# Second layer by Strassen's scheme, exp in eight pieces, and a written-out order, in a fused attention and two-layer kernel

## The chip, the cores and the metric

The kernel runs on one core of one Trainium2 chip. The metric is the device time in microseconds (us) of a launch; each kernel is run several times and the median is given.

## The reference

Attention in chunks of 64 tokens, then two dense layers with a leaky ReLU between them. 8 sequences of 576 tokens, 8 heads of 64; the layers take 4608 tokens of 512 features to 2048 and back to 512.

```python
def _attn_ref(q, k, v):                      # (8, 8, 576, 64)
    scores = scale * np.matmul(q_c, k_c.transpose(0, 1, 2, 4, 3))    # per chunk of 64 tokens
    scores = scores - np.max(scores, axis=-1, keepdims=True)
    attn = np.exp(scores)
    attn = attn / (np.sum(attn, axis=-1, keepdims=True) + 1e-09)
    out = np.matmul(attn, v_c)
...
def _moe_ref(x, w_in, w_out):                # (4608, 512), (512, 2048), (2048, 512)
    h = x @ w_in
    g = np.maximum(0.01 * h, h)
    return (g @ w_out).astype(np.float32)
```

Inputs and output are float32 in memory; on the chip everything that TensorE reads behind the first unit is 16-bit float (f16), and sums are float32.

## The kernel before, in words

The attention runs over 36 units of 128 tokens (two chunks, eight heads). A unit u passes through these stages, each a small function: queries and keys in transposed form (`stage_dq`, `stage_dk`: VectorE transposes 32x32 blocks of a tile loaded by POOL's queue, for units from 9 on; `stage_tq`, `stage_tk`, `stage_q`, `stage_k` before that), scores (`stage_s`: eight TensorE matmuls of 64 columns into the PSUM tile `Sp`, L342), row maximum (`stage_m`, VectorE, L351), subtraction of it (`stage_b`, VectorE, L355), one exp over all 512 elements (`stage_x`, ScalarE, L361), row sums, plus 1e-9 and reciprocal (`stage_z`, VectorE, L367 to L371), normalisation (`stage_n`, VectorE, L376), transposition (`stage_d`, a transposing DMA on SP's queue, L398, for units from 5 on), value matmuls (`stage_v`, eight of 64 columns, L409) and copy to `xT` (`stage_a`, ScalarE, L422).

The layers run over 17 blocks of tokens: eight of 128, four of 256, five of 512. The first layer (`mm1`) fills one PSUM bank of 512 columns for each chunk; `act1` takes it out through the leaky ReLU on ScalarE into `gT` (L181). The second layer (`mm2`) goes over tiles of 128 tokens, with 16 matmuls of 512 columns for each, in four chunks; `store` copies the tile out on ScalarE (L202) and sends it off on SP's queue. The last tile is split in three (`last`).

Every engine works through its instructions in the order in which the program issues them. That order is written out by hand: `FRONT` for the beginning (to unit 5), and then a loop in which each iteration issues the stages of several units, with chunks of the layers between them (`fill`; `QUARTERS` says how many). PSUM has eight banks: one for `Sp`, one each for `qp` and `kp` (the early transposes), one (`ox`) for the transposed weights and the values, and four (`mm`) that the layers rotate through.

Of the kernel before, what the change touches and what calls it, by code (L numbers as in the profile page):

```python
# [16 lines left out]
def kernel(  # L17
# [15 lines left out]
    CH = 64  # L33
# [8 lines left out]
    UD = 9  # L42
    UE = 5
    G = 2 * CH
# [13 lines left out]
    xT = sbp.tile([128, NT, n_tok], FP16, name="xT")  # L58
    qk: dict[int, tuple[bass.AP, bass.AP]] = {}

# [21 lines left out]

    qkd: dict[int, tuple[bass.AP, bass.AP]] = {}
# [67 lines left out]

    gT: dict[int, bass.AP] = {}
# [6 lines left out]
    def mm1(j, a):  # L159
# [3 lines left out]
        for i in range(nf):  # L163
            fc = nf * a + i
            for t in range(NT):
                nc.tensor.matmul(  # L166
                    out=hT[:, i, :],
                    lhsT=w_inT[:, t, fc * 128:(fc + 1) * 128],
                    rhs=xT[:, t, r0:r0 + tb],
                    start=(t == 0),  # L170
                    stop=(t == NT - 1),
                )
        HT[j, a] = hT

    def act1(j, a):
        tb = BLOCKS[j]
        nf = 512 // tb
        if j not in gT:
            tag, bufs, pad = ("gS", 4, 128) if tb == 128 else ("gT", 2, 512)
# [20 lines left out]
    def store(j, ti):  # L200
        osb = sbp.tile([128, d_model], FP32, name="osb", tag="osb", bufs=3)
# [4 lines left out]
    def last(j, ti):  # L206
        r0 = START[j] + ti * 128
        osb = sbp.tile([128, d_model], FP32, name="osb", tag="osb", bufs=3)
# [26 lines left out]

    chunks = []
    for j in range(len(BLOCKS)):
        chunks += c1(j) + c2(j)
    state = {"tokens": 0}

    def fill(n):
        for _ in range(n):
            if not chunks:
                return
            kind, j, a, p = chunks[0]
            if START[j] + BLOCKS[j] > state["tokens"]:
                return
            chunks.pop(0)
            if kind == "mm1":
                mm1(j, a)  # L250
                act1(j, a)
            elif j == len(BLOCKS) - 1 and a == BLOCKS[j] // 128 - 1:
                if p == 0:
                    last(j, a)
            else:
                mm2(j, a, p)
                if parts[j, a] == NFC // 4:
                    store(j, a)


# [97 lines left out]

    def stage_x(u):
# [5 lines left out]
    def stage_z(u):  # L365
        z = sbp.tile([128, 8], FP32, name="z", tag="z", bufs=2)
        nc.vector.tensor_reduce(out=z, in_=E[u], axis=AXL.X, op=ALU.add)  # L367
# [52 lines left out]
    def stage_a(u):  # L420
        xp = XP.pop(u)
        nc.scalar.activation(out=xT[:, :, u * G:(u + 1) * G], in_=xp, func=AFT.Copy, bias=0.0, scale=1.0)  # L422
# [17 lines left out]
    def finish(j):  # L440
        store(j, 0)
# [11 lines left out]
    def zero_act(i):  # L453
# [22 lines left out]
        "I": identity,  # L476
# [24 lines left out]
    def values(u):  # L501
        if 0 <= u < NU:
            do("v", u)
            do("a", u)

    QUARTERS = [5, 5, 5, 5, 5, 5, 6, 5, 6, 7, 6, 5, 9, 6, 7, 6, 6, 4, 6, 7, 5, 8, 7, 7, 9, 7, 4, 9, 4, 7, 7, 7, 7, 7, 7, 7, 7, 7, 7, 7, 7, 7, 7, 7, 7, 7, 7, 7, 7]
    for it in range(6, NU + 3):
        dve = UD <= it < NU
        if it <= NU:
            do("s", it - 1)  # L510
            do("m", it - 1)
            do("b", it - 1)
        if dve:
            stage_dq(it, 0)
        fill(2)
        if it - 3 >= UE:
            values(it - 3)
        if it <= NU:
            do("x", it - 1)
        if it - 2 < UE:  # L520
            do("e", it - 2)
            do("c", it - 2)
        if dve:
            stage_dq(it, 1)
            stage_dk(it)
        elif it < UD:
            do("tq", it)
            do("tk", it)
            both(it)
            do("k", it)  # L530
        if it <= NU:
            do("z", it - 1)
            do("n", it - 1)
            if it - 1 >= UE:
# [39 lines left out]
```

## Time and profile before

| | |
|---|---|
| median of 3 runs | 292.17 us (292.0 to 292.24) |
| span of the profiled execution | 290.8 us |
| time beyond the span (median less span) | 1.37 us |
| TensorE busy | 283.5 us, 97% of the span |
| VectorE busy | 178.4 us, 61% |
| ScalarE busy | 154.4 us, 53% |
| POOL busy | 118.5 us, 41% |
| mean granted TensorE clock | 0.994 |

The profile follows one execution; its own total time is not listed apart from the three runs, so the span stands beside their median. PE is TensorE's matmuls and PEld its weight loads, DVE is VectorE, ACT is ScalarE, SP and POOL are the engines whose queues issue most DMAs. A row of grouped instructions gives line, engine, operation, output and input tiles, shapes, count, busy time, the mean length of one in ns, and the idle time in front of them with what ended it. L166 is line 166 of the kernel before.

### The profile page before, as it was taken

How to read it: one execution, taken by the hardware profiler on the slowest of the kernel's cores; microseconds unless marked ns; L12 is line 12 of the kernel's file. 1: busy time of each engine (PE TensorE's matmuls, PEld its weight loads, DVE VectorE, ACT ScalarE, POOL GpSimd, SP SyncE). 2: the span in 40 equal slices, each digit the busy share in tenths (PEclk: the TensorE clock that was granted, in tenths of full speed). 3: DMA queues.
4: the chain of work that ended last, by engine and by line, in shares of the span. 5: the costliest groups of instructions: out<-in, count | busy, mean ns of one | idle time of the engine just before them, and what ended most of it. 6: DMA issues, size and time to landing. Idle time of an engine off the chain costs nothing.

```text
span 290.8 us, 6052 instructions
## 1 busy us (share of the span) xinstructions
PE 283.5 (97%) x2468; PEld 170.4 (59%) x2468; DVE 178.4 (61%) x333; ACT 154.4 (53%) x273; POOL 118.5 (41%) x148
## 2 busy tenths in 40 slices
PE   8789999999999999999999999999999999999995
PEld 4579945877776767667454444445454444444444
DVE  5866245778968899989776797987777520000000
ACT  6756524575564564555575347733773377126511
POOL 8748545697735944961393359500000000000000
PEclk9979999999999999999999999999999999999999
DMA  9999999999999999999599799993201210010012
GB/s 149 158 195 155 177 177 190 159 119 166 161 132 116 148 115 175 110 125 155 68 143 99 78 158 149 92 126 95 70 18 54 92 54 2 36 75 34 2 72 72
DMA packets 191580, 32.51 MB, mean 112 GB/s; under 512 B 182593, under 2 KB 187073, under 8 KB 191553
## 3 DMA queue, kind: packets, MB, share of 16 engines
q0 software_dynamic: 167136, 18.10, 119.3%
q1 hardware_dynamic: 23232, 13.70, 20.4%
q10 hardware_dynamic: 1184, 0.33, 0.5%
q8 instruction: 19, 0.31, 0.4%
q14 instruction: 9, 0.07, 0.1%
HBM read 36.70 MB, written 9.44 MB: 159 GB/s over the span
## 4 chain that ended last, share of the span: by engine, by line
PE 92%; DMA 3%; POOL 2%; issue 0%; DVE 0%; DVEq 0%; POOLq 0%
PE hT L166 43%; PE oP L191 42%; DMA w_inT<-in_moe_w_in_dram 3%; PE xp L409 3%; PE Sp L342 3%; PE oP L217 1%; POOL VB L103 1%; POOL k_in L79 1%; POOL q_in L79 1%; PE kp L276 0%; PE qp L276 0%; PE tpe L384 0%; POOL w_inT L110 0%; DVE osb L225 0%; POOL ident masks.py:199 0%
## 5 line engine op out<-in xcount | busy, mean ns | idle before, releaser
L166 PE MATMUL hT<-xT,w_inT 128*128 128x128 f16 (+2 forms) x1088 | 133.6, 279 | 0.4 <-DMA w_inT<-in_moe_w_in_dram 0.3
L191 PE MATMUL oP<-w_outT,gT 128*128 128x512 f16 x560 | 128.4, 379 | 0.0
L166 PEld LDWEIGHTS <-w_inT 128*128 128x128 f16 x1088 | 83.6, 98 | 38.4 <-issue 0.6
L181 ACT ACTIVATE gT<-hT 128x512 f16<-128x512 f32 x144 | 84.0, 598 | 35.6 <-PE hT L166 35.0
L191 PEld LDWEIGHTS <-gT 128*128 128x128 f16 x560 | 52.4, 98 | 56.5
L202 ACT ACTIVATE osb<-oP 128x512 f32<-128x512 f32 x35 | 20.9, 596 | 67.4 <-PE oP L191 62.5
L94 POOL DMA_DIRECT2D q_d<-in_q_dram x48 | 38.8, 822 | 33.3 <-DVE QZ L324 27.5
L351 DVE TENSOR_REDUCE mx<-Sp 128x8 f32<-128x512 f32 x36 | 24.8, 688 | 31.6 <-PE Sp L342 31.3
L94 POOL DMA_DIRECT2D k_d<-in_k_dram x48 | 38.9, 842 | 3.5 <-DMA q_d<-in_q_dram 3.0
L324 DVE STREAM_TRANSPOSE QZ<-q_d 64x512 f16<-64x512 f16 (+1 forms) x60 | 38.2, 644 | 0.4
L422 ACT ACTIVATE xT<-xp 128x512 f16<-128x512 f32 x36 | 21.4, 594 | 23.0 <-PE xp L409 23.0
L225 DVE COPY osb<-oP 128x128 f32<-128x128 f32 x1 | 0.3, 291 | 53.7 <-PE oP L217 53.7
L367 DVE TENSOR_REDUCE z<-ex 128x8 f32<-128x512 f16 x36 | 23.6, 656 | 5.4 <-ACT ex L361 5.1
L103 POOL DMA_DIRECT2D VB<-in_v_dram x16 | 18.5, 1172 | 18.1 <-PE xp L409 17.1
L376 DVE TENSOR_TENSOR en<-ex,zi 128x512 f16<-128x512 f16 x36 | 24.9, 691 | 1.2
L355 DVE TENSOR_TENSOR sh<-Sp,mx 128x512 f32<-128x512 f32 x36 | 24.8, 690 | 1.1
L361 ACT ACTIVATE ex<-sh 128x512 f16<-128x512 f32 x36 | 22.5, 626 | 1.1 <-DVE sh L355 1.1
L332 DVE STREAM_TRANSPOSE KT<-k_d 128x512 f16<-128x512 f16 (+1 forms) x30 | 19.4, 654 | 2.2 <-DMA k_d<-in_k_dram 1.4
L409 PEld LDWEIGHTS <-VB 128*128 128x128 f16 x288 | 13.2, 99 | 6.7 <-issue 0.9
L342 PEld LDWEIGHTS <-QZ 128*128 128x128 f16 x288 | 13.0, 99 | 6.9 <-DVE KT L332 0.8
L409 PE MATMUL xp<-et,VB 128*128 128x64 f16 x288 | 14.5, 194 | 0.8 <-ACT QZ L301 0.8
L342 PE MATMUL Sp<-KT,QZ 128*128 128x64 f16 x288 | 14.5, 194 | 0.0
(47 smaller groups left out, 102.5 us busy)
## 6 DMA issues: line engine op xcount, KB each, us to landing
out_dram<-osb SPq DMA_DIRECT2D x35, 256.0 KB, 3.2
VB<-in_v_dram POOLq DMA_DIRECT2D x16, 288.0 KB, 6.7
q_d<-in_q_dram POOLq DMA_DIRECT2D x48, 72.0 KB, 5.0
k_d<-in_k_dram POOLq DMA_DIRECT2D x48, 72.0 KB, 5.2
w_inT<-in_moe_w_in_dram POOLq DMA_DIRECT2D x8, 256.0 KB, 10.2
w_outT<-in_moe_w_out_dram POOLq DMA_DIRECT2D x4, 512.0 KB, 11.0
q_in<-in_q_dram POOLq DMA_DIRECT2D x7, 128.0 KB, 6.2
k_in<-in_k_dram POOLq DMA_DIRECT2D x7, 128.0 KB, 5.7
```

The source lines that it names most:

```text
L94: nc.gpsimd.dma_start(out=t[p0:p0 + 32, m, :, :, :].rearrange("p h b d -> p (h b) d"), in_=src[b, h0:h0 + 2, :, dh * 32:dh * 32 + 32].rear ...
L166: nc.tensor.matmul(out=hT[:, i, :], lhsT=w_inT[:, t, fc * 128:(fc + 1) * 128], rhs=xT[:, t, r0:r0 + tb], start=(t == 0), stop=(t == NT - 1),)
L181: nc.scalar.activation(out=gT[j][:, nf * a:nf * a + nf, :], in_=HT.pop((j, a)), func=AFT.Prelu, bias=0.0, scale=1.0, alpha=0.01)
L191: nc.tensor.matmul(out=o, lhsT=gT[j][:, fc, ti * 128:(ti + 1) * 128], rhs=w_outT[:, fc, :], start=(n == 0 and fc == part * 4), stop=(n == ...
L324: nc.vector.transpose(out=qz[s * CH:(s + 1) * CH, :, e0:e0 + n, s, :], in_=qkd[b][0][s * CH:(s + 1) * CH, :, at:at + n * CH].rearrange("p ...
L342: nc.tensor.matmul(out=Sp[:, i, :], lhsT=qz[:, 2 * m + g, e, :, :], rhs=kt[:, 2 * m + g, e, :], start=True, stop=True)
L351: nc.vector.tensor_reduce(out=MX[u], in_=SP[u], axis=AXL.X, op=ALU.max)
L355: nc.vector.tensor_tensor(out=SH[u], in0=SP.pop(u), in1=MX.pop(u).unsqueeze(2).to_broadcast((128, 8, CH)), op=ALU.subtract)
L361: nc.scalar.activation(out=E[u], in_=SH.pop(u), func=AFT.Exp, bias=0.0, scale=SCL)
L367: nc.vector.tensor_reduce(out=z, in_=E[u], axis=AXL.X, op=ALU.add)
L376: nc.vector.tensor_tensor(out=E[u], in0=ex, in1=ZI.pop(u).unsqueeze(2).to_broadcast((128, 8, CH)), op=ALU.mult)
L409: nc.tensor.matmul(out=xp[:, t, e, :], lhsT=VB[b % NVB][:, t, c, :], rhs=et[:, t // 2, e, t % 2, :] if u < UD else et[:, t % 2, e, t // 2, :],
```

## The change

The blocks become eight of 128 tokens and fourteen of 256. The second layer of 13 of them (`FAST`, blocks 8 to 20) goes by Strassen's scheme (in Winograd's form): the block's `gT` is cut into two halves of tokens and two halves of the 2048 features, `w_outT` into two halves of features and two of outputs. Seven products of 128 tokens x 1024 features x 256 outputs (eight matmuls of 256 columns each) take the place of eight. For that, VectorE makes four sums of halves of `w_outT` once (`weight_sum`), and four sums of halves of `gT` for each block (`token_sums`), all f16. Products 1, 6, 7 and 4 go through one PSUM bank (X, the former `qp`), 5 and 3 through another (Z, the former `kp`), 2 through one of the four `mm` banks (W). ScalarE copies the results of 1, 6 and 7 to SBUF and that of 4 to the output tile; VectorE adds 1 to 2, 7 to 5 and 6 to 3 into the output tile (`combine`). Products 6 and 7 add onto what the bank holds of product 1, product 4 onto that too, and 3 onto 5.

The matmuls of block j's products are mixed with the first layer of block j+1 (`MIXED`; 0 is a first-layer chunk, "sums" is a step without a matmul).

For units from 9 on (`UX`) `stage_b` and `stage_x` are replaced: `stage_nb` scales the maximum on VectorE (128x8), and `stage_f` does the exp in eight pieces of 64 elements on ScalarE, which read the scores from PSUM, take the scaled maximum as bias and give the row sums as a second output; the row-sum reduction in `stage_z` is left out for these.

`xT` holds 2048 tokens in place of all 4608 and is written round. The loop behind `FRONT` is replaced: each stage of each unit has a step at which it is issued (`T`, from `SPACE`, and the offsets `O_...`), and evictions, sums and combines follow their matmuls by an offset in steps (`D_...`), or are issued earlier where a matmul needs them (`flush`).

```diff
-    BLOCKS = [128, 128, 128, 128, 128, 128, 128, 128, 256, 256, 256, 256, 512, 512, 512, 512, 512]
+    BLOCKS = 8 * [128] + 14 * [256]
+    FAST = range(8, 21)
+    HF, HM = NFC // 2, d_model // 2
-    xT = sbp.tile([128, NT, n_tok], FP16, name="xT")
+    RING = 2048
+    xT = sbp.tile([128, NT, RING], FP16, name="xT")
...
+    def weight_sum(n):
+        b11, b12 = w_outT[:, :HF, :HM], w_outT[:, :HF, HM:]
+        b21, b22 = w_outT[:, HF:, :HM], w_outT[:, HF:, HM:]
+        x, y = {1: (b12, b11), 2: (b22, TW.get(1)), 3: (b22, b12), 4: (b21, TW.get(2))}[n]
+        TW[n] = sbp.tile([128, HF, HM], FP16, name=f"TW{n}")
+        nc.vector.tensor_tensor(out=TW[n], in0=x, in1=y, op=ALU.subtract)
+
+    def token_sums(j, n):
+        nh = BLOCKS[j] // 2
+        a11, a12 = gT[j][:, :HF, :nh], gT[j][:, HF:, :nh]
+        a21, a22 = gT[j][:, :HF, nh:], gT[j][:, HF:, nh:]
+        SG[j, n] = sbp.tile([128, HF, nh], FP16, name="SG", tag="gS", bufs=4, padded_shape=[128, HF, 256])
+        x, y, op = {
+            1: (a21, a22, ALU.add),
+            2: (SG.get((j, 1)), a11, ALU.subtract),
+            3: (a11, a21, ALU.subtract),
+            4: (a12, SG.get((j, 2)), ALU.subtract),
+        }[n]
+        nc.vector.tensor_tensor(out=SG[j, n], in0=x, in1=y, op=op)
+
+    def product(j, n, i):
+        nh = BLOCKS[j] // 2
+        g, w = gT[j], w_outT
+        where, left, right = {
+            1: ("X", g[:, :HF, :nh], w[:, :HF, :HM]),
+            2: ("W", g[:, HF:, :nh], w[:, HF:, :HM]),
+            3: ("Z", SG.get((j, 4)), w[:, HF:, HM:]),
+            4: ("X", g[:, HF:, nh:], TW.get(4)),
+            5: ("Z", SG.get((j, 1)), TW.get(1)),
+            6: ("X", SG.get((j, 2)), TW.get(2)),
+            7: ("X", SG.get((j, 3)), TW.get(3)),
+        }[n]
...
+        for f in range(HF):
+            nc.tensor.matmul(
+                out=to[:, i, :],
+                lhsT=left[:, f, i * 128:(i + 1) * 128],
+                rhs=right[:, f, :],
+                start=(j, where) not in opened,
+                stop=(f == HF - 1),
...
+    def combine(j, n):
...
+        if n in (1, 6, 7):
+            kept[j, n] = keep()
+            nc.scalar.activation(out=half(kept[j, n]), in_=half(bank[j, "X"]), func=AFT.Copy, bias=0.0, scale=1.0)
+            return
...
+        if n == 4:
+            nc.scalar.activation(out=to, in_=half(bank[j, "X"]), func=AFT.Copy, bias=0.0, scale=1.0)
+        else:
+            nc.vector.tensor_tensor(
+                out=to,
+                in0=half(bank[j, "W" if n == 2 else "Z"]),
+                in1=half(kept[j, {2: 1, 5: 7, 3: 6}[n]]),
+                op=ALU.add,
+            )
...
+    MIXED = (0, 1, 0, 2, 0, 5, 6, 0, 0, 7, 0, 0, 4, 0, 3)
...
+    D_G = 1.25
+    D_S = 2.75
+    D_K = 0.5
+    D_C = 0
+    D_O = 1
...
+    def stage_nb(u):
+        NB[u] = sbp.tile([128, 8], FP32, name="nb", tag="nb", bufs=2)
+        nc.vector.tensor_scalar_mul(out=NB[u], in0=MX.pop(u), scalar1=-SCL)
+
+    def stage_f(u, i0, i1):
...
+        for i in range(i0, i1):
+            nc.scalar.activation(
+                out=E[u][:, i, :],
+                in_=SP[u][:, i, :],
+                func=AFT.Exp,
+                bias=NB[u][:, i:i + 1],
+                scale=SCL,
+                accum_out=Z[u][:, i:i + 1],
+            )
...
     def stage_z(u):
-        z = sbp.tile([128, 8], FP32, name="z", tag="z", bufs=2)
-        nc.vector.tensor_reduce(out=z, in_=E[u], axis=AXL.X, op=ALU.add)
+        if u in Z:
+            z = Z.pop(u)
+        else:
+            z = sbp.tile([128, 8], FP32, name="z", tag="z", bufs=2)
+            nc.vector.tensor_reduce(out=z, in_=E[u], axis=AXL.X, op=ALU.add)
...
+    SPACE = [5, 5, 5, 5, 6.0, 7, 4.5, 6, 6, 6, 8.5, 8.0, 6.5, 8.5, 8.5, 8.0, 8.5, 7.0, 7.0, 10.0, 7.5, 8.5, 7.0, 7.5, 9.5, 6.5, 8.0, 8.0, 7.5, 10.0, 7.0]
...
+    T = {5: 0}
+    for u in range(6, NU):
+        T[u] = T[u - 1] + SPACE[u - 6]
+    at(3, "v", 4)
+    at(3, "a", 4)
+    for u in range(5, NU):
+        t = T[u]
+        if u >= UD:
+            at(t - O_Q, "dq", u, 0)
+            at(t - O_Q + O_R, "dq", u, 1)
+            at(t - O_Q + 2 * O_R, "dk", u)
...
+        at(t, "s", u)
+        at(t + O_M, "m", u)
...
+            at(t + O_M, "nb", u)
+            at(t + O_F, "f", u, 0, 4)
+            at(t + O_F + O_H, "f", u, 4, 8)
+            n = t + O_Z
+        for what in ("z", "n", "d"):
+            at(n, what, u)
+        w = t + (O_U if u < U_V else O_V)
+        at(w, "v", u)
+        at(w, "a", u)
+    for b in range(3, B):
+        at(T[9 * b // 2 - 5] - O_L, "D", b)
+    for n in range(4):
+        at(T[9 + n] + O_W, "W", n + 1)
```

The offsets that the prediction uses: `O_F` = 3 (exp), `O_Z` = 5 (row sums to transposed load), `O_U` = 13 for units below 14 and `O_V` = 15.5 from there on (value matmuls), `O_Q` = 6 (query and key transposes ahead of the scores), `O_W` = 8.5 (weight sums).

More of the change, by code (lines that the diff above doesn't have):

```diff
@@ L207, in last @@
         r0 = START[j] + ti * 128
-        osb = sbp.tile([128, d_model], FP32, name="osb", tag="osb", bufs=3)
+        osb = sbp.tile([128, d_model], FP32, name="osb", tag="osb", bufs=3, padded_shape=[128, 2 * d_model])
         for c0, c1, copy, queue in (
@@ L237 @@
     for j in range(len(BLOCKS)):
-        chunks += c1(j) + c2(j)
+        chunks += mixed(c1(j), j - 1) if j - 1 in FAST else c1(j)
+        if j not in FAST:
+            chunks += c2(j)
     state = {"tokens": 0}
[L241 to L258, printed above, removed]
+    events: list[tuple] = []
```

190 lines of the change are left out of this document (140 added, 50 removed).

## The prediction

> **What bounds the kernel now.** I read the page first: its busy times, the granted clock and the shares of the chain that ended last.
>
> ```profile
> span 290.8 us, 6052 instructions
> PE 283.5 (97%) x2468; PEld 170.4 (59%) x2468; DVE 178.4 (61%) x333; ACT 154.4 (53%) x273; POOL 118.5 (41%) x148
> PEclk9979999999999999999999999999999999999999
> PE 92%; DMA 3%; POOL 2%; issue 0%; DVE 0%; DVEq 0%; POOLq 0%
> ```
>
> TensorE is the bound, at full granted clock, and the chain hardly ever leaves it. An average may hide stretches, so the busy times by stretch come next (columns: stretch; length; PE, PEld, DVE, ACT, POOL busy with instruction counts; clock; DMA share; GB/s).
>
> ```profile
> 44.00:100.00 56.00, 56.00 (x638) 40.57 (x637) 43.26 (x82) 31.46 (x57) 38.42 (x47) 1.00 2.38 149
> 100.00:160.00 60.00, 60.00 (x494) 37.54 (x492) 51.01 (x93) 34.62 (x64) 33.96 (x41) 1.00 2.10 124
> 160.00:220.00 60.00, 60.00 (x418) 29.49 (x416) 49.32 (x90) 33.29 (x60) 17.52 (x20) 1.00 1.19 95
> 220.00:288.00 68.00, 67.87 (x388) 33.19 (x386) 9.61 (x20) 29.34 (x51) 0.00 (x0) 1.00 0.15 51
> ```
>
> From 44 to 288 us TensorE has no gap. VectorE is 82 to 85% busy from 100 to 220 us and nearly free after it; ScalarE stays below 60%. So a saved matmul saves its whole time, as long as VectorE and ScalarE keep up with a shorter schedule. The price of a matmul is its pitch, not its listed length (the 128x512 form is listed with 379 ns, but these overlap). The chain gives the pitch; the timeline row says which form the first chain row is.
>
> ```profile
> 113.05 1.91 PE L166 MATMUL hT<-xT,w_inT 128*128 128x256 f16 x16
> ```
> ```profile
> 113.22 1.75 PE hT L166 x16
> 157.25 3.45 PE oP L191 x16
> 160.71 0.23 PE Sp L342 x8
> 246.35 13.81 PE oP L191 x64
> 260.16 13.81 PE hT L166 x64
> ```
>
> 512 columns take 13.81/64 = 0.2158 us, 256 columns 1.75/16 = 0.1092 us, in both layers at the same rate; eight matmuls of a chunk's attention take 0.23 us.
>
> **TensorE's part.** Second layer: 13 blocks go from 32 matmuls of 512 columns to 7x8 = 56 of 256 columns. 416 x 0.2158 = 89.8 us become 728 x 0.1092 = 79.5 us: -10.3. First layer: the five blocks of 512 become ten of 256, 320 x 0.2158 = 69.1 us become 640 x 0.1092 = 69.9: +0.8. The matmul list of the changed kernel has 728 and 896 matmuls of 256 columns in the two layers, and the attention's and the last tile's are unchanged. Sum: -9.45 us. The profiled execution has a span of 290.8 us; the median run is 292.17, 1.37 us more, which I carry over. Without a stall: 281.35 + 1.37 = 282.7 us.
>
> **What that asks of the other two engines.** A step is one chunk of the written order: eight matmuls of 256 columns, 0.874 us (the four of 512 in the 128-token blocks: 0.863), or a "sums" step with no matmul. Sixteen steps make a block. Prices:
>
> ```profile
> L181 ACT ACTIVATE gT<-hT 128x512 f16<-128x512 f32 x144 | 84.0, 598 | 35.6 <-PE hT L166 35.0
> L324 DVE STREAM_TRANSPOSE QZ<-q_d 64x512 f16<-64x512 f16 x48 | 33.7, 701 | 0.4
> L376 DVE TENSOR_TENSOR en<-ex,zi 128x512 f16<-128x512 f16 x36 | 24.9, 691 | 1.2
> L355 DVE TENSOR_TENSOR sh<-Sp,mx 128x512 f32<-128x512 f32 x36 | 24.8, 690 | 1.1
> L351 DVE TENSOR_REDUCE mx<-Sp 128x8 f32<-128x512 f32 x36 | 24.8, 688 | 31.6 <-PE Sp L342 31.3
> L367 DVE TENSOR_REDUCE z<-ex 128x8 f32<-128x512 f16 x36 | 23.6, 656 | 5.4 <-ACT ex L361 5.1
> L361 ACT ACTIVATE ex<-sh 128x512 f16<-128x512 f32 x36 | 22.5, 626 | 1.1 <-DVE sh L355 1.1
> L422 ACT ACTIVATE xT<-xp 128x512 f16<-128x512 f32 x36 | 21.4, 594 | 23.0 <-PE xp L409 23.0
> L332 DVE STREAM_TRANSPOSE KT<-k_d 128x512 f16<-128x512 f16 x24 | 17.1, 711 | 2.2 <-DMA k_d<-in_k_dram 1.4
> L369 DVE TENSOR_SCALAR ze<-z 128x8 f32<-128x8 f32 x36 | 8.2, 229 | 1.2
> L371 DVE RECIPROCAL zi<-ze 128x8 f32<-128x8 f32 x36 | 7.3, 203 | 1.2
> L393 DVE COPY et<-tpe 128x512 f16<-128x512 f16 x4 | 1.7, 424 | 5.0 <-PE tpe L384 5.0
> L303 DVE CAST QZ<-qp 64x512 f16<-64x512 f32 x1 | 0.7, 683 | 1.6 <-ACT QZ L301 1.6
> L227 ACT ACTIVATE osb<-oP 128x256 f32<-128x256 f32 x1 | 0.4, 385 | 1.1 <-PE oP L217 1.1
> L225 DVE COPY osb<-oP 128x128 f32<-128x128 f32 x1 | 0.3, 291 | 53.7 <-PE oP L217 53.7
> L227 ACT ACTIVATE osb<-oP 128x128 f32<-128x128 f32 x1 | 0.3, 278 | 0.5 <-PE oP L217 0.5
> L136 ACT ACTIVATE one<-one 128x1 f16<-128x1 f16 x1 | 0.2, 206 | 0.0
> ```
> ```profile
> 152.74 0.69 DVE L351 TENSOR_REDUCE mx<-Sp 128x8 f32<-128x512 f32 x1 [1.15 <-PE Sp L342]
> 153.47 0.69 DVE L355 TENSOR_TENSOR sh<-Sp,mx 128x512 f32<-128x512 f32 x1
> ```
> ```profile
> 154.47 0.60 ACT L181 ACTIVATE gT<-hT 128x512 f16<-128x512 f32 x1 [0.27 <-PE hT L166]
> 154.96 0.59 ACT L422 ACTIVATE xT<-xp 128x512 f16<-128x512 f32 x1
> ```
>
> On VectorE the next start comes 0.04 us after an end (152.74 + 0.69 to 153.47); on ScalarE 0.11 us before it (154.47 to 154.96 for 0.60). I add or take these off.
>
> *The token sums* (f16 of f16 and f16, 1024 elements per partition) have no row. The 512- and 128-element copies of f32 (683 and 291 ns) give 1.02 ns per element and 160 ns fixed; the f16 copy of 512 (424 ns) runs at half that per element. So a sum lies between 0.69 and 1.21 us. The two `TENSOR_TENSOR` rows are at the full rate, but each has an f32 operand; the sums have none, as the f16 copy has none, so I take 0.69, pitch 0.73, and keep 1.25 as the other end. The four weight sums of 2048 elements: 1.25 or 2.29 pitch. [...] The combining add of 256 f32: 0.42, pitch 0.46.
>
> *The eight exp pieces* of 64 elements that also give sums. ScalarE's rows have a slope of (598-278)/384 = 0.83 ns, so 64 elements take 0.225 us. Low end: eight at an overlapped pitch of 0.115, 0.9 us. High end: none overlaps and each is followed by a read-out as long as the shortest row (206 ns): 8 x 0.431 = 3.45. I take no overlap and an overlapped read-out, 8 x (0.225 + 0.10) = 2.6, since each piece has two outputs and reads a per-partition bias. [...]
>
> Gone from VectorE for each of the 27 units from 9 on: the subtraction (0.73) and the sum reduction (0.70); new there: a small scaling, priced as `ze`, 0.27. A unit then costs VectorE mx 0.73, scaling 0.27, transposes 2 x 0.74 + 0.75, ze and zi 0.51, en 0.73: 4.47.
>
> Steady stretch, steps 63 to 222, by the placed order: 150 chunks, 20 units. TensorE 150 x 0.874 + 41 x 0.23 = 140.5 us. VectorE 20 x 4.47 - 1.1 (one key step and two query steps fall outside) + 40 sums x 0.73 + 30 combines x 0.46 = 131.3, 93%. ScalarE 80 x 0.49 + 21 x 0.48 + 40 copies of 256 x 0.28 = 60.5 and 20 exps: 79, 112 or 129 for 0.9, 2.6 or 3.45, at most 92%. TensorE stays the bound. Inside a block the tightest waits are the single accumulator bank for products 1, 6, 7 and 4 (ScalarE must empty it while two chunks, 1.75 us, run), and the third token sum before product 7; walked by these prices through block 14 (us after its first score step) they are ready 1 to 2 us early: third sum 5.6, product 7 at 7.7; copy of 7 out at 9.2, product 4 at 10.3; copy of 4 out at 13.4, the next product 1 at 14.3. VectorE's queue holds them behind ze of the unit, which waits for the last exp piece: up to 1 us, and the combines and token sums queue behind that; products 3 and 7 wait for those.
>
> Two early stretches are tighter. Steps 34 to 46: TensorE 9 x 0.874 + 4 x 0.863 + 4 x 0.23 = 12.2; VectorE 3 x (0.73 + 0.27 + 0.75) + 4 x 0.74 + 2 x 1.24 + 3 weight sums x 1.25 = 14.4, 2.2 too much. Steps 47 to 62: TensorE 14.0, VectorE 14.5, ScalarE 6.5 + 3 x 2.6 = 14.3. Buffers take part of that; I charge 1.5 us (0 to 2.7).
>
> The last term is the transposed load that feeds the value matmuls.
>
> ```profile
> DMA to landing us min/median/max: 4.2/5.5/6.5
> ```
>
> That is for 70 to 95 us. Units 9 to 13 have their value step 8 steps after ze: 8 x 0.874 + 2 x 0.23 = 7.5 us. The exp was placed two steps before ze and so ends some 1.35 us after that place (2.6 and 0.5 of queue, less 1.75); ze, zi, en 1.24; landing 5.5: 8.1 us, 0.6 late. A stall at one unit covers the next, so three of the five pay: 1.8 us (0 with the cheap exp; 5 with the dear one). Later units have 10.5 steps. Another 0.5 for the rest. The query and key loads keep their place, with the score step of unit 9b/2 - 5, and the value loads theirs, so POOL's queue is not moved past anything; the output stores stand in SP's queue between these loads but follow results that are ready before. Sum: 282.7 + 1.5 + 1.8 + 0.5 = **286.5 us**; the likeliest case's own range is 284 to 290.
>
> **Rivals.** *No stall* (chance 0.20): 282.7; for it speaks that VectorE's share averages 93%.
> *Dear exp* (0.18): at 3.45 the value step is 1.45 late (three times, 4.4), the steps 34 to 62 cost 3.5, tight blocks 0.4 four times: 9.5 us, 292.2, as before, 290 to 294. The one-element row of 206 ns speaks for it, the overlap of neighbours on ScalarE against.
> *VectorE becomes the bound* (0.12, slower): token sums at the full rate, as both `TENSOR_TENSOR` rows have it. Steady 131.3 + 40 x 0.52 = 152, 11.6 over TensorE; steps 34 to 46 5.3 over, 47 to 62 2.5: some 19 less 2 of cover, 300 us. It decides from a pitch of 1.05 us a sum: there the overruns add up to the 9.45 saved.
> Something else that I haven't priced, slower: 0.06. The forecast keeps 0.44.
>
> **Numbers.** Faster by over 0.2% (0.6 us, about what a measurement of this kernel tells from no change): 0.20 + 0.44 + 0.07 of the dear exp = 0.71; within: 0.04; slower 0.07 + 0.12 + 0.06 = 0.25. The range, 282.5 to 294, leaves out the last two, 0.18.
>
> **What would show it.** The 256-column second layer at 0.109 us a matmul; token sums at 0.69; the distance from one unit's first to last exp piece near 2.6; TensorE's gaps under 5 us in all, before xp of units 9 to 13 and in steps 34 to 62. It is wrong if the sums take 1.2, if ScalarE passes 95% in a steady block, or if gaps of TensorE return in each block before product 6 or 7.

## The result and the profile after

The changed kernel takes 287.51 us in the median (286.19 to 289.52), the kernel before 292.09 us (291.44 to 292.24): a ratio of 0.986, 95% interval 0.981 to 0.991. A second comparison, in new executions, gives 287.45 against 292.09, ratio 0.982 (0.979 to 0.985). The forecast was 286.5 us, in a range of 282.5 to 294. The profiled execution took 286.59 us with a span of 284.8 us. Executions more than 1.5% slower than the fastest of their kernel are left out of the medians below: two of six of sums_twice (300.71 and 303.20 us), one of five of d9_neither (290.58) and one of six of exp_first (289.50).

The page, the lines that answer to those shown of before:

```profile
span 284.8 us, 7841 instructions
PE 274.5 (96%) x3100; PEld 233.0 (82%) x3100; DVE 197.9 (70%) x401; ACT 203.4 (71%) x704; POOL 118.2 (41%) x148
PEclk9999999999999999999999999999999999999999
PE 69%; DMA 19%; POOL 7%; ACT 2%; issue 1%; DVE 1%; DVEq 0%; SPq 0%; POOLq 0%
```

TensorE's busy time fell by 9.0 us and VectorE's and ScalarE's rose by 19.5 and 49. The chain now leaves TensorE for 31% of the span, though TensorE is idle in only 4% of it: the chain runs back through the loads of the beginning. Where TensorE idles is told by the stretches (the same columns as before).

```profile
60.00:75.00 15.00, 13.07 (x161) 9.03 (x159) 10.18 (x20) 9.04 (x33) 10.79 (x15) 1.00 2.56 149
75.00:90.00 15.00, 13.63 (x161) 10.62 (x159) 11.74 (x23) 11.80 (x55) 8.67 (x11) 1.00 2.60 147
90.00:105.00 15.00, 14.25 (x164) 12.67 (x162) 14.11 (x29) 13.52 (x51) 9.99 (x13) 1.00 2.37 88
105.00:120.00 15.00, 15.00 (x163) 13.53 (x162) 13.06 (x26) 12.44 (x54) 7.62 (x10) 1.00 1.59 125
112.00:210.00 98.00, 98.00 (x1065) 88.51 (x1063) 79.61 (x167) 79.66 (x323) 45.52 (x54) 1.00 1.58 112
```

All of the loss lies between 60 and 105 us: 1.93 + 1.37 + 0.75 = 4.05 us. From there on TensorE has no gap, with VectorE and ScalarE at 81% each (79.61 and 79.66 of 98).

The prices, first by shape (busy us, mean ns of one, then the idle time before them), then two rows of the chain:

```profile
L201 PE MATMUL prX<-TW,SG 128*128 128x256 f16 x208 | 27.0, 273 | 0.0
L182 DVE TENSOR_TENSOR SG<-gT 128x1024 f16<-128x1024 f16 x26 | 17.4, 671 | 0.0
L524 ACT ACTIVATE ex<-Sp,nb 128x64 f16<-128x64 f32 x216 | 64.2, 333 | 0.5 <-DVE nb L516 0.5
L524 ACT ACTIVATION_READ_ACCUMULATOR ex<-Sp,nb 128x1 f32 x216 | 49.2, 228 | 0.0
L548 DVE TENSOR_SCALAR ze<-z 128x8 f32<-128x8 f32 x36 | 7.6, 212 | 16.1 <-ACT ex L524 15.7
```
```profile
68.62 2.47 ACT ex L524 x16
110.92 0.87 PE prW L201 x8
```

Eight matmuls of a Strassen product take 0.87 us, 0.109 each, the forecast price. A token sum takes 0.67 us. An exp piece is two rows, the piece itself (333 ns) and a read-out of its sum (228 ns); eight of both take 2.47 us, where the listed lengths add up to 4.49, so the read-outs overlap.

What ends the gaps between 60 and 105 us, from TensorE's timeline (start, length, the instructions, then the idle time before them and what ended it):

```profile
64.83 0.41 PE L494 MATMUL Sp<-KT,QZ 128*128 128x64 f16 x8 [1.47 <-DVE KT L484]
71.14 0.39 PE L494 MATMUL Sp<-KT,QZ 128*128 128x64 f16 x8 [0.37 <-ACT ex L524]
78.53 0.39 PE L588 MATMUL xp<-et,VB 128*128 128x64 f16 x8 [0.36 <-DMA et<-en]
85.62 0.41 PE L588 MATMUL xp<-et,VB 128*128 128x64 f16 x8 [1.00 <-DMA et<-en]
93.36 1.03 PE L256 MATMUL hT<-xT,w_inT 128*128 128x256 f16 x8 [0.69 <-ACT xT L602]
```

Five gaps, four kinds of cause: the key transpose of unit 9 (its load lands late), the score bank that the exp still reads, two transposed loads `et` in front of the value matmuls (units 9 and 10), and a copy that is queued on ScalarE.

The largest gap can be traced to the kernel before. These are unit 9's key transpose and scores, first before, then the key transpose after:

```profile
66.43 0.71 DVE L332 STREAM_TRANSPOSE KT<-k_d 128x512 f16<-128x512 f16 x1 [1.44 <-DMA k_d<-in_k_dram]
68.39 0.40 PE L342 MATMUL Sp<-KT,QZ 128*128 128x64 f16 x8
```
```profile
64.06 0.71 DVE L484 STREAM_TRANSPOSE KT<-k_d 128x512 f16<-128x512 f16 x1 [2.71 <-DMA k_d<-in_k_dram]
```

VectorE waited for the load before, too, but TensorE had 1.25 us of other work left when the transpose was done. Now the load lands 2.4 us earlier, and TensorE is ready for the scores 5.0 us earlier (64.83 less the gap of 1.47, against 68.39).

From the first matmul of the layers to the last end (18.99 to 287.87 us before, 17.48 to 281.83 after, by TensorE's timelines) the time is 268.9 us before and 264.35 after: 4.5 us less, that is the 9.45 forecast, less the 4.05 of gaps, less 0.9 in small pieces that I can't place. The span is 6.0 us shorter, since this execution also began its first matmul 1.5 us sooner; in the profiles of the variants below that start lies anywhere from 16.97 to 18.25 us, so I count it as scatter.

### The profile page after: what moved, and what is told of

It is laid out like the page before. It is cut to its first block, busy times and chain, and to the rows that moved or that the text cites. A ratio compares the mean times of both kernels' runs of the same rounds, so it can differ in the third digit from the quotient of the medians.

```text
span 284.8 us, 7841 instructions
## 1 busy us (share of the span) xinstructions
PE 274.5 (96%) x3100; PEld 233.0 (82%) x3100; DVE 197.9 (70%) x401; ACT 203.4 (71%) x704; POOL 118.2 (41%) x148
## 4 chain that ended last, share of the span: by engine, by line
PE 69%; DMA 19%; POOL 7%; ACT 2%; issue 1%; DVE 1%; DVEq 0%; SPq 0%; POOLq 0%
PE hT L256 34%; PE prX L201 16%; PE prZ L201 8%; DMA VB<-in_v_dram 5%; DMA et<-en 5%; PE prW L201 4%; DMA w_inT<-in_moe_w_in_dram 4%; DMA q_d<-in_q_dram 3%; DMA k_d<-in_k_dram 3%; PE xp L588 2%; PE Sp L494 2%; PE oP L281 2%; ACT ex L524 2%; POOL k_in L86 1%; PE oP L307 1%
## 5 line engine op out<-in xcount | busy, mean ns | idle before, releaser
L256 PE MATMUL hT<-xT,w_inT 128*128 128x256 f16 (+1 forms) x1408 | 143.4, 253 | 0.7 <-ACT xT L602 0.7
L256 PEld LDWEIGHTS <-w_inT 128*128 128x128 f16 x1408 | 115.4, 98 | 11.4 <-issue 0.8
L524 ACT ACTIVATE ex<-Sp,nb 128x64 f16<-128x64 f32 x216 | 64.2, 333 | 0.5 <-DVE nb L516 0.5
L524 ACT ACTIVATION_READ_ACCUMULATOR ex<-Sp,nb 128x1 f32 x216 | 49.2, 228 | 0.0
L201 PEld LDWEIGHTS <-SG 128*128 128x128 f16 x416 | 40.1, 98 | 4.5
L281 PE MATMUL oP<-w_outT,gT 128*128 128x512 f16 x144 | 33.5, 379 | 0.1
L226 DVE TENSOR_TENSOR osb<-prZ,keep 128x256 f32<-128x256 f32 x26 | 10.9, 418 | 23.6 <-ACT keep L217 14.9
L201 PE MATMUL prX<-TW,SG 128*128 128x256 f16 x208 | 27.0, 273 | 0.0
L217 ACT ACTIVATE keep<-prX 128x256 f32<-128x256 f32 x39 | 15.1, 386 | 11.2 <-PE prX L201 10.9
L182 DVE TENSOR_TENSOR SG<-gT 128x1024 f16<-128x1024 f16 x26 | 17.4, 671 | 0.0
```

The source lines that it names most:

```text
L201: nc.tensor.matmul(out=to[:, i, :], lhsT=left[:, f, i * 128:(i + 1) * 128], rhs=right[:, f, :], start=(j, where) not in opened, stop=(f == ...
L256: nc.tensor.matmul(out=hT[:, i, :], lhsT=w_inT[:, t, fc * 128:(fc + 1) * 128], rhs=xT[:, t, r0 % RING:r0 % RING + tb], start=(t == 0), sto ...
L281: nc.tensor.matmul(out=o, lhsT=gT[j][:, fc, ti * 128:(ti + 1) * 128], rhs=w_outT[:, fc, :], start=(n == 0 and fc == part * 4), stop=(n == ...
L524: nc.scalar.activation(out=E[u][:, i, :], in_=SP[u][:, i, :], func=AFT.Exp, bias=NB[u][:, i:i + 1], scale=SCL, accum_out=Z[u][:, i:i + 1],)
```

## Experiments

All times are medians, beside the kernel before on the same chip.

| kernel | median us (range) | before, same chip | ratio (95%) |
|---|---|---|---|
| as_changed | 287.45 (286.02 to 288.26) | 292.09 | 0.982 (0.979 to 0.985) |
| no_strassen | 300.00 (298.06 to 302.15) | 292.09 | 1.025 (1.021 to 1.029) |
| one_exp | 291.95 (290.65 to 293.52) | 292.09 | 1.000 (0.997 to 1.002) |
| late_both | 289.54 (287.49 to 291.20) | 292.09 | 0.990 (0.986 to 0.993) |
| direct9 | 286.98 (285.76 to 288.41) | 291.95 | 0.983 (0.979 to 0.986) |
| late_v | 287.19 (286.48 to 287.44) | 291.95 | 0.983 (0.980 to 0.986) |
| direct9_v | 287.41 (286.10 to 290.16) | 291.95 | 0.985 (0.981 to 0.989) |
| sums_twice | 296.45 (295.29 to 298.08) | 291.95 | 1.016 (1.012 to 1.019) |
| d9_nosums | 287.14 (285.87 to 288.78) | 291.61 | 0.986 (0.983 to 0.989) |
| d9_noload | 287.00 (286.30 to 287.44) | 291.61 | 0.984 (0.982 to 0.986) |
| d9_neither | 286.74 (286.20 to 286.98) | 291.61 | 0.983 (0.982 to 0.985) |
| exp_first | 286.49 (285.06 to 286.98) | 292.07 | 0.983 (0.979 to 0.986) |

### The changed kernel again, and without Strassen's scheme

> The changed kernel once more, for its spread and as the mate of the others. Its four runs lay between 286.2 and 289.5 us, with a mean granted clock that fell from 1.000 to 0.988 as the time rose. Theory (late loads for units 9 to 11 stop TensorE for some 4 to 5 us between 60 and 105 us, and in some executions longer): 286 to 290 again, and a slower execution has larger gaps in that stretch only. Rival (a lower clock spread over the whole run): the gaps of the slowest are no larger, and matmuls are longer elsewhere.

```diff
-    FAST = range(8, 21)
+    FAST = range(0)
```

> The 13 blocks go by the plain second layer (32 matmuls of 512 columns each, ScalarE stores), everything else as changed; steps in a block stay 16, so the placed order holds. The weight sums are still made, and not used. Theory (the gain is the matmuls alone): 89.8 - 79.5 = 10.3 us more of TensorE, the early gaps as they are: 287.5 + 10.3 = 297.8, between 296 and 299. Rival (the new order and the exp on ScalarE are worth something of themselves, Strassen less than its matmuls, since it loads VectorE): 292 to 294.

The changed kernel came out at 287.45, with executions from 286.02 to 288.26. Its clocks, 0.994 to 1.000, don't follow the times; whether its slower executions have larger gaps isn't shown, since only one execution was traced. Without the scheme it takes 300.0 us, 12.5 more, where the difference of the matmuls alone is 10.3. By shape, and by stretches, in this kernel:

```profile
L281 PE MATMUL oP<-w_outT,gT 128*128 128x512 f16 x560 | 129.7, 382 | 0.4
```
```profile
112.00:210.00 98.00, 97.70 (x840) 66.72 (x839) 52.83 (x110) 71.45 (x284) 45.45 (x54) 1.00 1.58 110
```

The 416 matmuls of 512 columns are back (560 instead of 144), and VectorE falls to 54%, but TensorE stays full: with the scheme gone there is nothing to win from the freer engines. So the scheme is worth its matmuls, and the other two parts of the change, taken alone (the weight sums are still made), make this kernel 8 us slower than the kernel before. In the profiled execution a dip of the granted clock, which the last section shows, costs 1.7 us; but the two executions with clocks of 0.999 and 1.000 took 299.75 and 300.15 us, so the dip doesn't explain the extra 2.2 us of the median. I have not placed them.

### One exp for all heads

```diff
-    UX = 9
+    UX = 36
```

> All units take the subtraction, one exp and the sum reduction as before; Strassen and the placed order stay. VectorE gets 0.73 + 0.70 - 0.27 = 1.16 us more per unit, ScalarE 2.5 - 0.6 = 1.9 less. Theory (VectorE is within a tenth of being the bound and the exp split is what makes room): from the prediction's prices VectorE needs 154 us for the 140 of steps 63 to 222: 8 to 17 us more, 296 to 304. Rival (VectorE waits 15.7 us for the exp pieces, and these waits go with the split): 286 to 290, no loss.

291.95 us, 4.5 more than the changed kernel, level with the kernel before, and between the two ranges expected. By stretches:

```profile
60.00:80.00 20.00, 17.81 (x218) 13.31 (x215) 14.66 (x26) 9.47 (x17) 17.51 (x20) 0.91 2.67 142
80.00:100.00 20.00, 16.65 (x186) 13.30 (x183) 19.41 (x35) 11.00 (x20) 10.27 (x13) 1.00 2.10 119
100.00:120.00 20.00, 18.66 (x206) 16.56 (x205) 19.45 (x37) 9.95 (x21) 6.97 (x9) 1.00 1.40 100
140.00:200.00 60.00, 60.00 (x658) 54.21 (x656) 58.02 (x111) 35.01 (x68) 28.97 (x35) 1.00 1.91 116
```

Subtraction and sum reduction are back on VectorE, and TensorE loses 2.2, 3.4 and 1.3 us in the first three stretches. The first of these is the gap for unit 9's key again, with VectorE at 73% (the changed kernel's second profile, further down, loses 2.6 us there); what is new in it is a clock of 0.91. In the other two, where the changed kernel loses 1.1 and nothing, VectorE is at 97%. But from 140 to 200 us VectorE is just as full (58.02 of 60) and TensorE has no gap at all. So it is mainly up to some 140 us that the split exp pays; from there to 200 us VectorE could carry the rest of that work too. By the prediction's prices, 0.73 + 0.70 - 0.27 = 1.16 us more per unit, it would have been overfull there: 131.3 + 20 x 1.16 = 154.5 us of work in 140.5. Its prices were too high, and the reason can be read in the changed kernel's timeline of VectorE:

```profile
96.63 0.69 DVE L555 TENSOR_TENSOR en<-ex,zi 128x512 f16<-128x512 f16 x1
97.24 0.70 DVE L476 STREAM_TRANSPOSE QZ<-q_d 64x512 f16<-64x512 f16 x1
```

The transpose starts 0.08 us before the listed end of the instruction ahead (96.63 + 0.69 = 97.32). The prediction took 0.04 us after the end for every instruction, from a pair of which the second reads what the first writes. In VectorE's timeline from 112 to 210 us all such pairs start 0.02 to 0.04 us after the listed end; of the other neighbours without a wait about two thirds start before it, mostly by 0.06 to 0.09 us.

### Every token sum twice

```diff
-        nc.vector.tensor_tensor(out=SG[j, n], in0=x, in1=y, op=op)
+        for _ in range(2):
+            nc.vector.tensor_tensor(out=SG[j, n], in0=x, in1=y, op=op)
```

> Every token sum is made twice into the same tile: 4 more VectorE instructions of 0.67 us in each of the 13 blocks. By the prediction's prices this is a token sum with a pitch of 1.25 or more, its slower rival: 300 us. Theory now (between 112 and 210 us VectorE is busy 81%, and instructions without a dependence start 0.08 us before the one ahead ends, so a sum costs some 0.6 us of the queue): 81% + 2.4 of 14.06 us = 98%, TensorE nearly undisturbed: 287 to 290.

This asks the prediction's slower rival directly: a token sum then costs 2 x 0.67 us, above the 1.05 at which VectorE was to become the bound. 296.45 us, 9 more than the changed kernel. Stretches, and TensorE's longest waits in the whole execution (us in total, times, longest):

```profile
100.00:120.00 20.00, 18.77 (x203) 16.53 (x201) 18.57 (x37) 16.03 (x67) 5.50 (x6) 1.00 1.05 89
140.00:200.00 60.00, 57.49 (x609) 50.91 (x606) 56.51 (x114) 46.73 (x187) 27.97 (x34) 1.00 1.52 104
```
```profile
PE xp L589 <- DMA et<-en: 4.1, 6, 1.2
PE prX L202 <- DVE SG L183: 2.9, 7, 0.8
```

TensorE now loses time all the way (2.5 us from 140 to 200), and waits for the token sums, as the rival had it, though longer in total for transposed loads. VectorE is at 94%, lower than in one_exp, which loses nothing in this stretch. So here a busy share does not say when VectorE becomes the bound. A likely reason is VectorE's own waits: from 140 to 200 us `ze` still waits 1.4 us for the last exp pieces here, and what is queued behind that wait can't use the time, while one_exp has no such wait; this was not tested by itself. The expectation written ahead of this run, that there was room left, was wrong; the prediction's condition fits, but a sum of 1.05 us, where it put the turn, was not run.

### Where the early gaps come from: moving steps

The gaps between 60 and 105 us are the only lost time, so eight kernels went to them. Their base is the second profile of the changed kernel (as_changed), by stretches:

```profile
60.00:80.00 20.00, 17.45 (x236) 12.93 (x234) 13.65 (x26) 12.70 (x48) 15.20 (x18) 1.00 2.77 138
80.00:100.00 20.00, 18.89 (x206) 15.06 (x203) 17.85 (x36) 16.93 (x68) 14.38 (x18) 1.00 2.56 132
```

Here 3.66 of 40 us are lost. The first kernel places unit 9's scores 1.5 steps later, for the late key load, and the value steps of unit 9 one step and of unit 10 one and a half steps later, for the late transposed loads; that of unit 11 comes one and a half steps earlier. Unit 9's transposes and row sums keep their place, its exp comes half a step earlier, and the first weight sum stays where it was:

```diff
-    SPACE = [5, 5, 5, 5, 6.0, 7, ...
+    SPACE = [5, 5, 5, 6.5, 4.5, 7, ...
...
-            at(t - O_Q, "dq", u, 0)
-            at(t - O_Q + O_R, "dq", u, 1)
-            at(t - O_Q + 2 * O_R, "dk", u)
+            o = 7.5 if u == 9 else O_Q
+            at(t - o, "dq", u, 0)
+            at(t - o + O_R, "dq", u, 1)
+            at(t - o + 2 * O_R, "dk", u)
...
-            at(t + O_F, "f", u, 0, 4)
-            at(t + O_F + O_H, "f", u, 4, 8)
-            n = t + O_Z
+            o = 1.0 if u == 9 else O_F
+            at(t + o, "f", u, 0, 4)
+            at(t + o + O_H, "f", u, 4, 8)
+            n = t + (3.5 if u == 9 else O_Z)
...
-        w = t + (O_U if u < U_V else O_V)
+        w = t + {9: 12.5, 10: 14.5, 11: 11.5}.get(u, O_U if u < U_V else O_V)
...
-        at(T[9 + n] + O_W, "W", n + 1)
+        at(T[9 + n] + (O_W if n else 7.0), "W", n + 1)
```

> The changed kernel with a few places moved: scores of unit 9 one and a half steps later (its exp, normalisation and transposed load stay where they were), value step of unit 9 half a step to one step later, of unit 10 one and a half later, of unit 11 one and a half earlier. Theory (TensorE's gaps are four late operands: keys of unit 9, transposed weights of units 9 and 10, the copy of unit 11's values before the first chunk of block 9; it has other chunks to run meanwhile): 2.5 to 3.5 us less than as changed, about 284.5. Rival (the loads limit the beginning, and a gap that is filled comes back at the next unit): within 0.5 us of as changed.

289.54 us, 2 more than the changed kernel. The waits between 55 and 110 us, and the clock behind the longest (TensorE alone: stretch; length; busy with count; clock; DMA share; GB/s):

```profile
ACT ex L524 <- DVE nb L516: 4.2, 1, 4.2
DVE KT L484 <- DMA k_d<-in_k_dram: 4.0, 1, 4.0
PE Sp L494 <- ACT ex L524: 3.4, 3, 2.5
```
```profile
73.00:76.00 3.00, 2.08 (x13) 0.72 2.46 177
76.00:79.00 3.00, 3.00 (x18) 0.72 3.03 133
```

The key transpose held VectorE for 4.0 us, at its old place (3.5 us in the base). The scores now come later, and with them the small scaling that the exp needs; the exp stands half a step earlier, ahead of the evictions, and held ScalarE for 4.2 us with these behind it. So unit 10's scores waited 2.5 us for the score bank, more than the 1.9 us that the move was to fill. Behind that gap the clock fell, and 3 x 0.28 twice is another 1.7 us. The one execution at a full clock took 287.49 us, the median of the changed kernel; the other five, with mean clocks of 0.994 and 0.988, took 289.40 to 291.20. So most of the 2 us may be the clock, which one execution does not settle.

The second removes the key load's part in another way: unit 9 takes the way of the units before it, plain loads and TensorE transposes, so that no key load behind VectorE's queue is waited for. The third only moves the value steps of units 10 (later) and 11 (earlier), the fourth does both.

```diff
-    UD = 9
+    UD = 10
...
-        "g2 g1 g3 v0 Q0 Q1 Q2 g4 Q3 g5 P1 P2 P0 P3 g6 v1 g7 g8 D2 "
+        "g2 g1 g3 v0 Q0 Q1 Q2 g4 Q3 g5 P1 P2 P0 P3 g6 v1 g7 g8 g9 D2 "
```

> Unit 9 takes its queries and keys the way units 6 to 8 do (a load of its own ahead of batch 2 on POOL's queue, eight TensorE transposes, copies on VectorE and ScalarE) in place of the batch of sequence 2; all else as changed. Theory (TensorE stands 1.6 to 1.9 us ahead of the scores of unit 9 because the last keys of batch 2 land too late, and where that gap trips the clock it costs 1.7 us more): the gap goes, 0.45 us of transposes come: 285 to 286, with a spread below 1.5 us, no stretch behind 60 us with a clock below 0.95. Rival (the beginning is limited by what the loads move, and the gap comes back at unit 10): 287 to 288, the same spread.

```diff
-        w = t + (O_U if u < U_V else O_V)
+        w = t + {10: 14.5, 11: 11.5}.get(u, O_U if u < U_V else O_V)
```

> Only the value steps of units 10 (one and a half steps later) and 11 (one and a half earlier) are moved. Theory (each gap stands by itself, since TensorE has other chunks): the 0.69 us ahead of the first chunk of block 9 goes and, where it occurs, the wait for the transposed weights of unit 10 (0 to 1.0 us): 286 to 287, the spread as it is because unit 9's gap remains. Rival (what is filled comes back later): 287.5.

> Both moves together: unit 9 by its own load, value steps of units 10 and 11 moved. Theory (independent gaps): 284 to 285, the best so far, spread below 1.5 us. Rival (one gap's filling is the next one's wait): as the better of the two alone.

286.98, 287.19 and 287.41 us: none is clear of the changed kernel's 287.45, and none of another. In direct9's profile:

```profile
60.00:100.00 40.00, 36.23 (x437) 28.16 (x435) 31.22 (x62) 30.26 (x116) 30.57 (x37) 1.00 3.01 138
```
```profile
PE xp L588 <- DMA et<-en: 2.1, 2, 1.6
```

The wait for the key is gone, 1.9 us in the base, and TensorE is busy for 36.23 of the 40 us where the base has 36.34. The time went into the wait for the transposed loads, 0.2 us in the base and 2.1 here. In late_v it is the other way round: none of the loads is waited for, and the key wait is 2.1 us. With both edits the profile shows 37.11, and the time doesn't follow. So these gaps are not separate prices: where one was cleared, another wait of the same stretch grew.

### Is it VectorE's weight sums, or the loads beside?

Two suspects for what paces that stretch: VectorE, which also makes four weight sums there (1.19 us each), and the traffic of the batch loads of queries and keys that fly beside the transposed loads. On direct9, one kernel leaves out the weight sums, one the load of sequence 3 (its units then take sequence 2's data), one both, so part of the computation is missing in each.

```diff
-        TW[n] = sbp.tile([128, HF, HM], FP16, name=f"TW{n}")
-        nc.vector.tensor_tensor(out=TW[n], in0=x, in1=y, op=ALU.subtract)
+        TW[n] = x
```

> Unit 9 by its own load, and the four weight sums left out: the products that would read them read halves of the second weight matrix, so part of the computation is missing. VectorE gets 4.8 us less between 60 and 95 us. With unit 9's own load alone the gap ahead of its scores went, but as much came back before 100 us. Theory A (VectorE and ScalarE are overfull in steps 14 to 62, as the prediction had it for steps 34 to 62, and that is what the gaps come to): 2 to 3 us less than with unit 9's load alone, 284 to 285. Theory B (what the loads move limits it): 286.5 to 287.5, as before.

```diff
     def load_qk_batch(b):
+        if b == 3:
+            qkd[3] = qkd[2]
+            return
```

> Unit 9 by its own load, and the batch load of sequence 3 (16 DMAs on POOL's queue, issued from 60 to 77 us) left out: units 13 to 17 read the queries and keys of sequence 2, so part of the computation is missing. Theory A: 286.5 to 287.5. Theory B (the transposed loads of units 8 to 11 take 5 to 7 us because this batch shares the DMA engines): they land in 2.4 to 4 us, TensorE's gaps between 60 and 100 us fall below 1.5 us: 284 to 285.

> Both left out, weight sums and the batch load of sequence 3, with unit 9 by its own load. Theory A: as without the weight sums. Theory B: as without the load. If both have a part, below either: 283 to 284, near the 282.7 without any stall, plus 0.45 for unit 9's transposes.

287.14, 287.00 and 286.74 us, against 286.98 for direct9: nothing. The stretch, in the three kernels in this order:

```profile
60.00:100.00 40.00, 37.15 (x444) 28.96 (x442) 28.41 (x60) 31.24 (x122) 31.36 (x38) 1.00 2.61 144
```
```profile
60.00:100.00 40.00, 37.19 (x445) 29.18 (x443) 31.84 (x61) 31.44 (x122) 19.11 (x22) 1.00 1.98 121
```
```profile
60.00:100.00 40.00, 36.66 (x442) 28.74 (x440) 26.25 (x58) 30.77 (x118) 19.10 (x22) 1.00 2.05 122
```

In the last VectorE is 5 us less busy than in direct9 (26.25 against 31.22 of 40) and TensorE is no fuller than with one part left out. So the weight sums are not what paces the stretch, and that suspect falls. On what the traffic costs the runs don't decide: with one batch left out POOL issued the next one sooner (at 75.6 us in place of 85.5), and what the DMA engines moved fell only from 138 to 121 GB/s. But they show a transposed load that landed sooner with less moved beside it. It is unit 9's, issued at 71.8 us in direct9 and at 71.6 in d9_noload:

```profile
DMA to landing us min/median/max: 6.2/6.2/6.2
```
```profile
DMA to landing us min/median/max: 2.4/2.4/2.4
```

From 72 to 76 us 134 GB/s were moved beside it in direct9, and 51 in d9_noload; d9_neither has 53 GB/s and 2.4 us too. The wait in front of unit 9's value matmuls, 0.44 us in direct9, is gone in both. The next transposed load is issued when the batch of sequence 4 is under way, takes 7.6 us (7.9 in direct9), and TensorE waits 1.56 us for it, as in direct9 (1.55).

### The loop through the exp

A third suspect is a loop: exp of a unit, normalisation on VectorE, transposed load, value matmuls, their copy by ScalarE, and then, behind that copy in ScalarE's queue, the exp of the unit two places later (unit 7's value step falls on the step of unit 9's exp, unit 8's one step ahead of unit 10's). If a load is late, the copy waits, and the next exp with it. The last kernel places the value step of units 7 to 10 a quarter step behind the exp of the unit two later, so that a late load holds no exp, and that of unit 11 earlier; it has direct9's edit too.

```diff
-        w = t + (O_U if u < U_V else O_V)
+        w = T[u + 2] + O_F + 0.25 if 7 <= u <= 10 else t + 11.5 if u == 11 else t + (O_U if u < U_V else O_V)
```

> As with both moves (unit 9 by its own load, value step of unit 11 one and a half steps earlier), and the value step and copy of units 7 to 10 placed just behind the exp of the unit two further on, in place of just ahead of it. Theory C (a loop limits the beginning: exp of a unit, normalisation 1.2 us, transposed load 6 to 8 us, value matmuls, copy on ScalarE, and only behind that copy, in ScalarE's order, the exp of the unit two further on; 12 us for two units, as long as their steps take, so whatever is filled elsewhere comes back): with the exps ahead of the waiting copies, the gaps between 60 and 100 us fall from 3 to 4 us to below 2 us, 285 to 286. Rival (the loads or TensorE's own order limit it): 287 again.

286.49 us in the median, and the shortest single execution of all, 285.06. Stretches, and a row of TensorE's timeline:

```profile
60.00:80.00 20.00, 20.00 (x259) 14.71 (x257) 16.50 (x32) 16.08 (x65) 15.62 (x19) 1.00 2.65 150
80.00:100.00 20.00, 17.38 (x193) 14.63 (x189) 16.91 (x32) 16.08 (x70) 15.17 (x19) 1.00 2.62 133
```
```profile
95.87 0.41 PE L588 MATMUL xp<-et,VB 128*128 128x64 f16 x8 [1.43 <-DMA et<-en]
```

The stretch from 60 to 80 us is full for the first time, and the lost time is 2.62 us where the base has 3.66; it lies from 80 to 100 us, again in front of value matmuls for the most part. Theory C had less than 2 us, so it is not borne out: direct9_v, d9_nosums and d9_noload, without this order, lose 2.8 to 2.9 us in the same stretch, which one profile of each can't tell from 2.62. The edit also gives unit 9's value step 3.25 more steps of time, so a fuller stretch up to 80 us need not come from the order on ScalarE. Against the changed kernel the median is 1.0 us shorter, but on another chip, and the ratios to the kernel before, 0.983 and 0.982, are the same: that it is a faster kernel is not shown. Whether the landing time of the transposed loads sets the remaining 2.6 us stays open: d9_noload freed one load of the traffic, and no run freed them all.

## Why the prediction was right, and where it was not

**TensorE's 9.45 us: right.** 0.87 us for eight matmuls of 256 columns, and no_strassen shows that without them nothing is gained. They are not enough alone: one_exp has them too, and is level with the kernel before. The scheme saves the time, and the split exp makes room on VectorE for it up to some 140 us.

**The bounded prices: right.** The token sum came out at 0.67 us against 0.69 forecast (other end 1.21), the eight exp pieces at 2.47 against 2.6 (ends 0.9 and 3.45). A sum of 1024 f16 elements is listed with 671 ns, where the f32 rows of before gave 1.21 us: less the 160 ns fixed that is 0.50 ns an element, as in the f16 copy of before (0.52), so that row was the right one to price it from. For the exp the 0.10 us that the forecast adds to each piece was an estimate of mine, which no run shows as such: the piece itself is listed with 333 ns against the 225 of the slope, its read-out with 228, and of these 561 ns some 250 are overlapped, which leaves 0.31 a piece against 0.325 forecast. What makes a piece 108 ns longer than the slope is not shown. Two rivals, the dear exp and the token sums at the full rate, fell with these rows, and the row in the changed kernel was enough to see it.

**The steady stretch: right in its result, wrong in its working.** No gap from 105 us on, as forecast. But VectorE was priced at 93% and measures 81%: the step that failed is "On VectorE the next start comes 0.04 us after an end", which holds for a dependent pair and was applied to all. From 112 to 210 us that is 0.04 for each of 167 instructions, 6.7 us, which a busy share doesn't count; and the listed lengths add up to 86.1 us where VectorE is busy for 79.6, so overlaps take off another 6.5. (The 1.1 us that the sum takes off for a key and two query transposes would be 2.2 by its own prices, which leaves 93%.) It did no harm here, because both values leave TensorE the bound. one_exp shows the error's size: from 140 to 200 us the 1.16 us more a unit, by the prediction's prices, are carried without a stall.

**The stalls: right in sum, in part in place, wrong in kind.** Forecast 1.5 + 1.8 + 0.5 = 3.8 us, in steps 34 to 62 and before the value matmuls of units 9 to 13. Measured: 4.05 us of gaps, all between 60 and 105 us; but the two ahead of the scores of units 9 and 10, 1.47 + 0.37 us, lie at steps 20 and 26, before the places forecast. By terms:
- late transposed loads: 1.8 forecast, three times 0.6 with every load landing in 5.5 us; 1.36 measured (0.36 + 1.00), for units 9 and 10, whose loads took 6.0 and 7.4 us;
- VectorE and ScalarE overfull: 1.5 forecast. As a load on VectorE it did not show: leaving out its weight sums changed nothing (d9_nosums). The waits for the score bank and for ScalarE's copy, 0.37 + 0.69 = 1.06, are the nearest thing to it;
- the rest, 0.5 forecast: the key of unit 9 alone costs 1.47. The prediction held that the loads "keep their place" and so priced them at nothing. The load did keep its place; the scores moved. By TensorE's timelines the scores of units 5 to 9 followed each other every 5.1 to 6.6 us before (44.40 to 68.39 us) and are placed five steps apart now, every 5.0 to 5.3 us (42.72 to 63.36, had unit 9's not waited), while the load lands only 2.4 us earlier.

That the sum still fits is partly luck: in the experiments the lost time shifts between these names, so they are not three terms to be added; what paces the stretch as a whole stays open.

**The slower rival: its mechanism is borne out, its threshold was not tested.** sums_twice puts a sum at 2 x 0.67 us, above the rival's 1.05, and gives 296.45 us, where the rival had 300 at 1.25 a sum.

## What to carry to other kernels

When steps are placed closer together, look at every load that feeds them: here the last key loads ahead of unit 9's scores took no less than before (6.1 to 6.7 us from issue to landing before, 6.5 to 7.2 after), so a lead of 1.25 us became a wait of 1.47, though nothing about the loads was edited. Price an engine's queue with the pitch of dependent neighbours and of others apart (on VectorE here 0.02 to 0.04 us after the listed end, and mostly 0.06 to 0.09 before it), and then ask what stands behind its waits: from 140 to 200 us TensorE lost 2.5 us with VectorE 94% busy (sums_twice) and none with 97% (one_exp). Before counting a gap as time to be won, clear it once and see whether another wait takes its place: here five kernels that each cleared one or more came out level (286.49 to 287.41 us against 287.45).

## What the runs showed of the hardware beyond what I expected

**Three of six gaps of 2.04 to 2.47 us were followed by a lower granted clock, down to 0.50.** TensorE's busy time and granted clock in short stretches (columns: stretch; length; PE busy with count; clock; DMA share; GB/s), first in one_exp, then in the changed kernel on the same chip:

```profile
64.00:67.00 3.00, 0.95 (x12) 1.00 2.12 205
67.00:70.00 3.00, 3.00 (x19) 0.57 2.98 131
70.00:73.00 3.00, 3.00 (x54) 0.87 2.61 130
```
```profile
64.00:67.00 3.00, 1.09 (x13) 1.00 2.10 204
67.00:70.00 3.00, 3.00 (x43) 1.00 2.85 137
```

The gap in one_exp, 2.19 us by TensorE's timeline, is followed by 0.57 and 0.87 of the clock, 3 x 0.43 + 3 x 0.13 = 1.7 us of lost work, more than three quarters of the gap again. In no_strassen the same place shows 0.50 and 0.93, behind a gap of 2.04. In the changed kernel a gap of 1.91 us, at the same place, is followed by the full clock. In all the traces taken here, three of the six gaps from 2.04 to 2.47 us that came later than 20 us were followed by such a dip (2.04 in no_strassen, 2.19 in one_exp and 2.47 in late_both; lowest clocks 0.50, 0.57 and 0.72), three were not (2.09 in late_v and in d9_neither, 2.43 in one_exp), and no shorter one was. So gaps of nearly one length were followed by a dip in some executions and not in others, and what decides it is not shown. The clock may also explain part of the spread of the first four times: with spans of 284.4, 284.8, 286.6 and 287.7 us and mean clocks of 1.000, 0.998, 0.994 and 0.988, the missing share of the clock times the span comes to 0, 0.6, 1.7 and 3.4 us, an estimate, and what is left is 284.2 to 284.9 in all four. In later runs it fits less well (as_changed: 285.5 us at 1.000, 284.8 at 0.994).

**The sum output of an ACTIVATE is an instruction of its own.** Each exp piece is followed by a read-out listed with 228 ns, two thirds of the piece; overlapped, eight pieces and eight read-outs take 2.47 us, 0.31 each for 64 elements.
